# Earlier raw weights, earlier second operands, a later unpacking of w_out and a deeper fetch of c in a fused attention and two-MLP kernel

## The chip, the cores and the metric

The kernel runs on one core of a Trainium2 chip. The metric is the device time of one execution in microseconds (us), the median of several runs. Before the change it is 904.29 us over three runs (901.79 to 904.33); the execution that the profiler recorded took 901.62 us, of which 899.8 lie between its first and its last instruction.

## The reference

Three stages stand behind one another, all in float32: attention inside chunks of 64 tokens, an MLP with a leaky activation, and a bilinear MLP.

```python
scores = scale * q_c @ k_c.T                      # per chunk of 64, head size 64
x = softmax(scores) @ v_c                         # -> (2304 tokens, 512)
h = x @ w_in                                      # w_in  512 x 2048
x2 = (maximum(h, 0) + alpha * minimum(h, 0)) @ w_out      # 2048 x 512
a = x2 @ w_a;  b = x2 @ w_b                       # each 512 x 1536
out = (a * b) @ w_o                               # 1536 x 512
```

The weights arrive as 64-bit floats and are brought to 32 bits on the chip ("unpacked").

## The kernel before

**Precision.** Every float32 operand is held as two tiles, a high part (`h` at the end of the name) that ScalarE rounds and a low part (`l`) that VectorE gets by subtraction (`to_hi` L83, `to_lo` L86). A product of two operands is three matmuls: high x high, high x low, low x high.

**Stages.** The 2304 tokens are five blocks: four of 512 and one of 256. For each block, attention runs beside MLP1 of the block before it. MLP1 goes through 16 slabs j of 128 hidden columns: `s1` (12 matmuls), the activation `prelu`, and two slabs later `s2` (12 matmuls into four accumulators). At the end of a block `end1` stores the result x2 to DRAM, save for the last block, whose result stays in PSUM.

Then comes the middle stage, a = x2 w_a, b = x2 w_b and c = a*b, for 12 slabs j of 128 columns. The four blocks of 512 make two pairs, p=0 and p=1. For a pair and a slab, `pair_group` (L595) gets the four products of two blocks and two weights from seven half-size products (42 matmuls of 512 columns into three PSUM banks, psA, psB, psD) instead of eight. For that it needs sums of the token tiles, `s1` to `s4`, for each pair (`sums`, `summed`), and differences of the weight tiles, `tT`, for each slab (`weights_steps` L513, which also unpacks the two raw tiles of w_a and w_b). The block of 256, the "rest", goes through `rest_group` (24 matmuls of 256 columns into psr). Below, (p,j) is a pair group and r j a rest group. Their order is a list (`seq`, L1021): (0,0) r0 (0,1) (1,0) r1 (1,1), then (0,j) r j (1,j) for each j, and at the end (0,11) (1,11) r11. Each result c goes to DRAM.

Last comes MLP2 (L1047 on): block after block, 12 slabs each, c is loaded back, split into high and low, and multiplied with the split w_o (`s4`, three matmuls for each 128 tokens).

**What sets the order.** Every engine works through its own list in the order in which the code is written; nothing is reordered at run time. Work that is not tied to a matmul (unpacking, splitting, sums) stands in one list, `todo2`. `background(us)` takes steps from its front until their written costs reach `us`; it is called inside the loops of MLP1's last block (with the budgets `BG`, L668), twice in each pair group (2.7 and 1.2) and once in each rest group (2.0). `need` takes steps until a mark is passed. The steps for the middle stage's first operands run in MLP1's last block (`before_mlp2`), together with the unpacking of all 12 slabs of w_o (`p_steps`), whose result goes to DRAM (`pd`) and comes back just before MLP2 (`wp..l<-pd`, L1043). The second pair needs the result of the last block, so its sums can only begin after MLP1 (`late_pair`, L771).

**Buffers.** Raw weights (512 KB each), the differences `tT` and the copies out share three buffers (`stg`). 72 tiles of 128x512 (`w`) hold nearly all else. c comes back into tiles of the pools `gh` and `gl` with three buffers each. All loads and stores are issued by SyncE (SP) in one order; a store that waits for its data, or a load that waits for its buffer, holds up all that stand behind it.

Of the kernel before, what the change touches and what calls it, by code (L numbers as in the profile page):

```python
# [8 lines left out]
F32 = mybir.dt.float32  # L9
# [9 lines left out]
def chunk_attention_prelu_mlp_bilinear_mlp(  # L19
# [77 lines left out]
    units += [("p", j) for j in range(J2)] + [(m, j) for j in range(J2) for m in "ab"]  # L97
# [368 lines left out]
    X, T = {}, {}  # L466
# [14 lines left out]
    def sums(p, kk, a21, a22):  # L481

        def src(q):
            return X[p, q][kk][1].bitcast(F32)
# [28 lines left out]
    def weights_steps(j):  # L513


        th, tl = xtiles("T")
        T[j] = th.rearrange("p k n -> p (k n)"), tl.rearrange("p k n -> p (k n)")
        ua, ub = (units.index((m, j)) for m in "ab")
        gen, t = {}, {}

# [11 lines left out]
        def tt(q, a, b):  # L532
            if "t" not in t:
                t["t"] = sp.tile([P, 2 * DM], F32, tag="stg", name="tT")
            nc.vector.tensor_tensor(  # L535
                out=t["t"][:, q * Q:(q + 1) * Q], in0=a(), in1=b(), op=ALU.subtract
            )
# [4 lines left out]
        def hi(c, m):  # L542
            to_hi(T[j][0][:, c], None, t[m])

        def lo(c, m):
            to_lo(T[j][0][:, c], T[j][1][:, c], t[m])

        ca, cb, ct = slice(0, DM), slice(DM, 2 * DM), slice(2 * DM, 4 * DM)
# [5 lines left out]
            (0.0, lambda: hi(ca, "a")),  # L554
            (0.69, lambda: end(ub, "b")),
            (0.0, lambda: hi(cb, "b")),
            (0.4, lambda: tt(0, part("b", 0), part("a", 0))),
            (0.4, lambda: tt(1, part("b", 1), part("t", 0))),
            (0.4, lambda: tt(2, part("b", 1), part("b", 0))),
            (0.4, lambda: tt(3, part("a", 1), part("t", 1))),  # L560
            (0.0, lambda: hi(ct, "t")),
            (0.69, lambda: lo(ca, "a")),
            (0.69, lambda: lo(cb, "b")),
            (1.2, lambda: lo(ct, "t")),
        ]

# [98 lines left out]
    U_P = NU1  # L665
    U_AB = NU1 + J2
    early2 = {}
    BG = [0.0, 0.0] + [2.6] * 12 + [6.0, 6.0]  # L668
# [9 lines left out]
    def p_steps(j):  # L678
        i = U_P + j
        gen = {}  # L680

        def begin():
            w_dma(i + 2)
            gen[0] = unpack_ops(i, True)
            next(gen[0])
# [10 lines left out]
    def before_mlp2():  # L696
# [8 lines left out]
        def first():  # L705
            w_dma(U_P + 2)
# [18 lines left out]

        def rest_in():
# [11 lines left out]
        def p_next():  # L738
            todo2.extend(p_steps(done["p"]))
            done["p"] += 1  # L740

        done["p"] = 0
        for j in range(1, 13):
            early2.setdefault(j, []).append(p_next)
        early2[1].insert(0, first)
        for j, fn in (
            (3, lambda: sums_at(0)), (4, lambda: sums_out(0)), (5, lambda: sums_at(1)), (6, lambda: sums_out(1)),
            (8, lambda: directs(0, ("11",))), (9, lambda: directs(0, ("12",))), (10, lambda: directs(0, ("22",))),
            (11, rest_in),
            (11, lambda: (w_dma(U_AB + 2), todo2.extend(weights_steps(0)))),  # L750
            (13, lambda: (fetch(1, "11", b3, 0), fetch(1, "12", b3, 1))),
        ):
            early2[j].append(fn) if j in early2 else early2.update({j: [fn]})
# [17 lines left out]
    def late_pair(acc):  # L771
# [4 lines left out]
        steps = []  # L776
        for kk in range(2):

            def a22(kk=kk):
                t["a22", kk] = a = wtile("a22", F32)  # L780
                nc.scalar.activation(out=a, in_=acc[2 + kk], func=AF.Copy)

            t[kk], four = sums(1, kk, lambda kk=kk: acc[kk], lambda kk=kk: t["a22", kk])
            steps += [(0.0, a22)] + four
        for kk in range(2):
            steps += summed(1, kk, t[kk])
        for kk in range(2):
            hi, lo = X[1, "22"][kk]
            steps += [
# [316 lines left out]
```

## Time and profile before

| what | value |
|---|---|
| median of three runs | 904.29 us (901.79 to 904.33) |
| the profiled execution | 901.62 us, its span 899.8 us |
| PE (TensorE) busy | 864.0 us, 96% of the span |
| DVE (VectorE) busy | 525.9 us, 58% |
| ACT (ScalarE) busy | 373.5 us, 42% |
| mean granted clock of TensorE | 0.985 of full speed |

The page divides the span in 40 slices of 22.5 us; PE is full in nearly all of them:

```profile
PE   7899999999999999999996899999999969999997
PEclk9999999999999999999997999999999999999999
```

Each digit is the busy share of a slice in tenths. The slices that fall short are the first ones (attention before there is any MLP work), slices 22 and 23 (the change from MLP1 to the middle stage, 472 to 517 us), slice 33 (the change to MLP2, about 742 us) and the last. A matmul of 512 columns starts 0.227 us after the one before it at full clock and 0.43 us at half clock.

### The profile page before, as it was taken

What the parts mean: (1) busy time and instruction counts of PE and PEld (TensorE: products, weight loads), DVE (VectorE), ACT (ScalarE), POOL (GpSimd) and SP (SyncE); (2) the same over time, 40 slices, a digit from 0 to 9 for tenths busy, and PEclk for the clock granted to TensorE, in tenths of its full rate; (3) what the DMA queues carried; (4) which work ended last, traced back from release to release, by engine and by line L of the source; (5) the groups of instructions that cost most, each with busy time, mean ns of one, the idle gap of its engine ahead of it and who ended that gap; (6) DMA issues with size and microseconds to landing.
All of it is one profiled execution on the core that took longest, in us unless ns stands there. A gap on an engine that the chain in (4) does not pass through costs nothing. (4 is left out here: it accounts for less than half of the span.)

```text
span 899.8 us, 13238 instructions
## 1 busy us (share of the span) xinstructions
PE 864.0 (96%) x5154; PEld 717.5 (80%) x5154; DVE 525.9 (58%) x976; ACT 373.5 (42%) x668; POOL 0.7 (0%) x6
## 2 busy tenths in 40 slices
PE   7899999999999999999996899999999969999997
PEld 6778889988888888888774688888888858888885
DVE  5999955454434443468777677777777672322322
ACT  5687766555435433346542222222222232222222
POOL 0000000000000000000000000000000000000000
PEclk9999999999999999999997999999999999999999
DMA  9686767464425220544420523333232163434433
GB/s 212 211 249 196 211 165 176 106 162 120 116 49 162 61 59 1 187 171 165 156 77 23 168 94 105 101 101 100 100 101 76 54 217 85 146 96 142 141 91 119
DMA packets 148702, 114.12 MB, mean 127 GB/s; under 512 B 96544, under 2 KB 121120, under 8 KB 148640
## 3 DMA queue, kind: packets, MB, share of 16 engines
q1 hardware_dynamic: 148352, 113.02, 42.5%
q8 instruction: 40, 0.66, 0.3%
q10 hardware_dynamic: 288, 0.26, 0.1%
q14 instruction: 22, 0.18, 0.1%
HBM read 70.79 MB, written 34.08 MB: 117 GB/s over the span
## 5 line engine op out<-in xcount | busy, mean ns | idle before, releaser
L387 DVE SCALAR_TENSOR_TENSOR pos<-neg,nalpha_sb,pos 128x512 f32<-128x512 f32 (+1 forms) x80 | 55.6, 695 | 106.3 <-ACT pos L386 106.1
L87 DVE TENSOR_TENSOR cl<-cl,ch 128x512 fp32r<-128x512 f32 (+1 forms) x60 | 38.3, 639 | 109.1 <-ACT ch L84 103.8
L84 ACT ACTIVATE ch<-cl 128x512 fp32r<-128x512 f32 (+1 forms) x60 | 35.3, 589 | 109.4 <-DMA cl<-cd 73.2
L87 DVE TENSOR_TENSOR gl<-pos,gh 128x512 fp32r<-128x512 f32 (+1 forms) x80 | 51.0, 638 | 43.5 <-ACT gh L84 43.5
L84 ACT ACTIVATE gh<-pos 128x512 fp32r<-128x512 f32 (+1 forms) x80 | 47.2, 590 | 64.6 <-DVE pos L387 64.6
L603 DVE TENSOR_TENSOR t<-p,psB 128x512 f32<-128x512 f32 x48 | 32.8, 684 | 56.7 <-PE psB L573 55.1
L385 ACT ACTIVATE neg<-psh 128x512 f32<-128x512 f32 (+1 forms) x80 | 43.8, 547 | 35.6 <-PE psh L367 35.4
L137 DVE SCALAR_TENSOR_TENSOR wx<-wx,wz 128x512 int32<-128x512 int32 x68 | 46.7, 687 | 13.8 <-ACT wx L125 11.0
L125 ACT ACTIVATE wx<-raw 128x512 f32<-128x512 f32 x68 | 43.1, 670 | 22.7 <-DMA raw<-in_moe_w_a_dram 10.9
L607 ACT ACTIVATE p<-psA 128x512 f32<-128x512 f32 x24 | 14.3, 596 | 76.0 <-PE psA L573 75.3
L386 ACT ACTIVATE pos<-psh 128x512 f32<-128x512 f32 (+1 forms) x80 | 44.2, 552 | 0.0
L129 DVE TENSOR_SCALAR wz<-raw 128x512 uint16<-128x512 uint16 x68 | 31.3, 460 | 16.7 <-DMA raw<-in_moe_w_a_dram 9.5
L613 ACT ACTIVATE p<-psD 128x512 f32<-128x512 f32 x24 | 14.3, 597 | 47.7 <-PE psD L573 45.6
L134 DVE TENSOR_SCALAR wz<-raw 128x512 uint16<-128x512 uint16 x68 | 30.8, 453 | 0.0
L367 PE MATMUL psr<-xrh,Tl 128*128 128x256 f32 x96 | 27.2, 283 | 0.0
L367 PE MATMUL psr<-xrl,Th 128*128 128x256 f32 x96 | 27.2, 283 | 0.0
L367 PE MATMUL psr<-xrh,Th 128*128 128x256 f32 x96 | 27.1, 283 | 0.0
L243 ACT ACTIVATE kqd<-kq 128x1024 uint16<-128x1024 uint16 x24 | 23.9, 1047 | 0.3 <-DMA kq<-in_k_dram 0.3
L641 ACT ACTIVATE b_sb<-psr 128x256 f32<-128x256 f32 x12 | 4.6, 384 | 41.2 <-PE psr L367 41.2
L84 ACT ACTIVATE Th<-wx 128x512 fp32r<-128x512 f32 x24 | 15.1, 630 | 12.2 <-DVE wx L137 12.2
L84 ACT ACTIVATE xh<-psSO 128x256 fp32r<-128x256 f32 x28 | 8.9, 384 | 25.0 <-PE psSO L343 25.0
L84 ACT ACTIVATE Th<-tT 128x1024 fp32r<-128x1024 f32 x12 | 12.7, 1062 | 14.8 <-DVE tT L535 14.8
(534 smaller groups left out, 2560.1 us busy)
## 6 DMA issues: line engine op xcount, KB each, us to landing
raw<-in_moe_w_out_dram SPq DMA_DIRECT2D x28, 512.0 KB, 3.8
cl<-cd SPq DMA_DIRECT2D x48, 256.0 KB, 2.6
raw<-in_moe_w_in_dram SPq DMA_DIRECT2D x16, 512.0 KB, 5.0
raw<-in_moe_w_a_dram SPq DMA_DIRECT2D x12, 512.0 KB, 3.8
raw<-in_moe_w_b_dram SPq DMA_DIRECT2D x12, 512.0 KB, 3.6
cd<-t SPq DMA_DIRECT2D x24, 256.0 KB, 2.0
cd<-p SPq DMA_DIRECT2D x24, 256.0 KB, 2.0
v<-in_v_dram SPq DMA_DIRECT2D x16, 256.0 KB, 4.4
```

Source lines behind the costliest of these rows:

```text
L84: nc.scalar.activation(out=hi, in_=src, func=AF.Copy)
L87: nc.vector.tensor_tensor(out=lo, in0=src, in1=hi.bitcast(F32), op=ALU.subtract)
L125: return nc.scalar.activation(out=x.bitcast(F32), in_=hw.bitcast(F32), func=AF.Copy, scale=2.0 ** -112)
L129: yield nc.vector.tensor_scalar(out=z2[:, :, 0], in0=h2[:, :, 1], scalar1=13, scalar2=None, op0=ALU.logical_shift_right)
L134: yield nc.vector.tensor_scalar(out=z2[:, :, 1], in0=h2[:, :, 3], scalar1=1 << 15, scalar2=None, op0=ALU.bitwise_and)
L137: yield nc.vector.scalar_tensor_tensor(out=x, in0=x, scalar=3, in1=z, op0=ALU.logical_shift_left, op1=ALU.bitwise_or)
L243: nc.scalar.activation(out=d, in_=src.bitcast(U16).rearrange("p (f t) -> p t f", t=2), func=AF.Copy)
L367: nc.tensor.matmul(out=ps, lhsT=a, rhs=b, start=(i == 0 and first), stop=(i == n_i - 1 and a is wl))
L385: nc.scalar.activation(out=neg, in_=h, func=AF.Relu, scale=-1.0)
L386: yield nc.scalar.activation(out=pos, in_=h, func=AF.Relu)
L387: yield nc.vector.scalar_tensor_tensor(out=pos, in0=neg, scalar=nalpha_sb[:, j:j + 1], in1=pos, op0=ALU.mult, op1=ALU.add)
L603: nc.vector.tensor_tensor(out=out, in0=a, in1=b, op=op)
```

## The change

Six things are changed.

- The order in which weights are asked for (`units`) puts w_a and w_b of slabs 0 and 1 first; the 12 tiles of w_o stand between later pairs. So w_o is unpacked in the middle stage, after each (1,j), one or two tiles each, and no longer in MLP1's last block. Raw weights are asked for one slab further ahead.
- `weights_steps` is cut in two: `weights_raw` (unpacking and differences) and `weights_in` (the splits). The differences are two tiles of 512 columns in the pool `w`; they were one of 1024 in `stg`. Slab 1 gets its first half in MLP1's last block and its second half before MLP1's last products (L1012 on).
- The second pair's tokens that lie in DRAM (11 and 12) are loaded into tiles of their own (`xraw`) and split in MLP1's last block; before, after the middle stage had begun.
- `late_pair` does all of its first half (kk=0) before the second.
- In `seq`, r10 moves behind (1,11).
- c is loaded four tiles ahead, not two, into the pool `w`, and the first four loads stand between the loads of w_o.

```diff
-    units += [("p", j) for j in range(J2)] + [(m, j) for j in range(J2) for m in "ab"]
+    units += [(m, j) for j in range(2) for m in "ab"]
+    n_p = 0
+    for j in range(2, J2):
+        units += [("a", j), ("b", j)]
+        upto = min(J2, -(-(j - 1) * J2 // (J2 - 3)))
+        units += [("p", i) for i in range(n_p, upto)]
+        n_p = upto
...
-            if "t" not in t:
-                t["t"] = sp.tile([P, 2 * DM], F32, tag="stg", name="tT")
+            if q % 2 == 0:
+                t["t", q // 2] = wtile("tT", F32)
...
+    def weights_in(j):
+        names = ("a", "b", ("t", 0), ("t", 1))
...
+        return [(0.0, begin)] + stagger([
+            [(0.0, lambda i=i: to_hi(*args(i))), (0.69, lambda i=i: to_lo(*args(i)))] for i in range(4)
+        ])
...
-    BG = [0.0, 0.0] + [2.6] * 12 + [6.0, 6.0]
...
+        def raw_in():
+            for q, half in (("11", 0), ("12", 1)):
+                operand(1, q)
+                for kk in range(2):
+                    raw1[q, kk] = wtile("xraw", F32)
+                    nc.sync.dma_start(out=raw1[q, kk], in_=x2d[b3][:, 2 * half + kk])
+        def raw_out():
+            todo2.extend(stagger([settled(1, q, kk, raw1[q, kk]) for q in ("11", "12") for kk in range(2)]))
...
-        for j in range(1, 13):
-            early2.setdefault(j, []).append(p_next)
...
+            (2, first), (3, lambda: sums_at(0)), (4, lambda: sums_at(1)), (5, lambda: w_dma(NU1 + 2)),
+            (5, lambda: sums_out(0)), (6, lambda: sums_out(1)),
+            (7, lambda: directs(0, ("11",))), (8, lambda: directs(0, ("12",))), (9, lambda: directs(0, ("22",))),
+            (9, lambda: todo2.extend(weights_steps(0))), (10, lambda: w_dma(NU1 + 4)),
+            (11, raw_in), (11, rest_in), (12, raw_out),
+            (13, lambda: todo2.extend(weights_raw(1))),
...
-                    background(BG[j] if j < len(BG) else 9.0)
+                    background(2.8 if j < J1 - 1 else 3.4)
             x = nxt
+        w_dma(NU1 + 6)
+        flush(1)
         background(99.0)
-        w_dma(U_AB + 4)
         mark((0, 0))
-        todo2.extend(weights_steps(1))
+        todo2.extend(weights_in(1))
         mark((0, 1))
-        background(3.0)
+        background(99.0)
         flush(0)
         late_pair(acc[0])
         mark((1, 0))
         mark((1, 1))
+        todo2.extend(weights_raw(2))
...
-        for j in range(2, J2 - 1):
+        for j in range(2, J2 - 2):
             seq += [(0, j), ("r", j), (1, j)]
-        seq += [(0, J2 - 1), (1, J2 - 1), ("r", J2 - 1)]
+        for j in (J2 - 2, J2 - 1):
+            seq += [(0, j), (1, j)]
+        seq += [("r", J2 - 2), ("r", J2 - 1)]
...
+                todo2.extend(weights_in(j + 2))
+                mark((0, j + 2))
+                i = units.index(("b", j + 2)) + 1
+                while i < len(units) and units[i][0] == "p":
+                    w_dma(i + 1)
+                    todo2.extend(p_steps(units[i][1]))
+                    i += 1
+                w_dma(i + 2)
             if (p, j) == (0, J2 - 1):
                 for i in range(J2):
                     W["p", i] = hl = wtile(f"wp{i}h"), wtile(f"wp{i}l")
                     nc.sync.dma_start(out=hl[1].bitcast(F32), in_=pd[i])
+                    if i < AHEAD:
+                        load_c(i)
...
-            load_c(i + 2)
+            load_c(i + AHEAD)
```

On VectorE, between the last evacuation of (0,1) and the first one of (1,0), the program before had these rows; `ss` and `a` are the sums and a copied token tile, `x1..l` low parts of the second pair; (1,0)'s first evacuation comes next.

```order
L87 TENSOR_TENSOR x1s1l<-ss_5154,x1s1h 128x512
L87 TENSOR_TENSOR x1s2l<-ss_5156,x1s2h 128x512
L87 TENSOR_TENSOR x1s3l<-ss_5158,x1s3h 128x512
L87 TENSOR_TENSOR x1s4l<-ss_5201,x1s4h 128x512
L87 TENSOR_TENSOR x1s1l<-ss_5205,x1s1h 128x512
L87 TENSOR_TENSOR x1s2l<-ss_5207,x1s2h 128x512
L87 TENSOR_TENSOR x1s3l<-ss_5209,x1s3h 128x512
L87 TENSOR_TENSOR x1s4l<-ss_5232,x1s4h 128x512
L87 TENSOR_TENSOR x122l<-a_5152,x122h 128x512
L87 TENSOR_TENSOR x122l<-a_5203,x122h 128x512
L87 TENSOR_TENSOR x111l<-x111l,x111h 128x512 x2
L87 TENSOR_TENSOR x112l<-x112l,x112h 128x512 x2
```

In the same place the changed program has five of these fourteen splits, and then (1,0)'s first evacuation.

```order
L87 TENSOR_TENSOR x1s1l<-ss_5129,x1s1h 128x512
L87 TENSOR_TENSOR x1s2l<-ss_5131,x1s2h 128x512
L87 TENSOR_TENSOR x1s3l<-ss_5133,x1s3h 128x512
L87 TENSOR_TENSOR x1s4l<-ss_5135,x1s4h 128x512
L87 TENSOR_TENSOR x122l<-a_5127,x122h 128x512
L614 TENSOR_TENSOR t_5185<-p_5177,psB 128x512
```

Four of the nine others (x111l, x112l) now stand in MLP1's last block, and five (the first half, kk=0) behind (0,0) and in r0.

On SyncE, between the stores of (1,3) and those of (1,4), the program before had the following; `cd_3` and `cd_4` are stores of c for slabs 3 and 4, the last number being a buffer.

```order
L442 DMA cd_3_138<-p_5752 128x512
L108 DMA raw<-in_moe_w_a_dram 128x4x256
L108 DMA raw<-in_moe_w_b_dram 128x4x256
L442 DMA cd_4_91<-t_5826 128x512
L442 DMA cd_4_115<-p_5818 128x512
L442 DMA cd_4_103<-b_sb 128x256
L442 DMA cd_4_127<-t_5939 128x512
```

Now two raw tiles of w_o stand ahead of the pair of raw weights, and the two stores to `pd` stand among the stores of c.

```order
L448 DMA cd_3_138<-p_5691 128x512
L111 DMA raw<-in_moe_w_out_dram 128x1024 x2
L114 DMA raw<-in_moe_w_a_dram 128x4x256
L114 DMA raw<-in_moe_w_b_dram 128x4x256
L448 DMA cd_4_91<-t_5775 128x512
L448 DMA cd_4_115<-p_5767 128x512
L448 DMA cd_4_103<-b_sb 128x256
L699 DMA pd_151<-wx 128x512
L448 DMA cd_4_127<-t_5892 128x512
L448 DMA cd_4_139<-p_5884 128x512
L699 DMA pd_152<-wx 128x512
```

The second of the raw pair takes the buffer that the first raw tile of w_o leaves. On SyncE after the last store of (0,11), the loads for MLP2 were, before:

```order
L442 DMA cd_11_122<-p_7061 128x512
L1043 DMA wp0l<-pd_147 128x512
L1043 DMA wp1l<-pd_148 128x512
L1043 DMA wp2l<-pd_149 128x512
L1043 DMA wp3l<-pd_150 128x512
L1043 DMA wp4l<-pd_151 128x512
```

and are now:

```order
L448 DMA cd_11_122<-p_7071 128x512
L1068 DMA wp0l<-pd_147 128x512
L1040 DMA cl<-cd_0_87 128x512
L1068 DMA wp1l<-pd_148 128x512
L1040 DMA cl<-cd_1_88 128x512
L1068 DMA wp2l<-pd_149 128x512
L1040 DMA cl<-cd_2_89 128x512
L1068 DMA wp3l<-pd_150 128x512
L1040 DMA cl<-cd_3_90 128x512
L1068 DMA wp4l<-pd_151 128x512
```

`wp3l` was the fourth load and is the seventh; the first loads of c stood behind the stores of (1,11) and r11.

## Rows read from the trace of the kernel before

**Rows 1.** By stage: start:end, length, busy PE, PEld, DVE, ACT, POOL; clock, DMA, GB/s.

```profile
45.00:460.00 415.00, 412.05 (x2823) 345.75 (x2822) 247.46 (x487) 224.77 (x412) 0.00 (x0) 1.00 0.49 139
460.00:520.00 60.00, 47.83 (x213) 38.39 (x212) 41.86 (x71) 18.98 (x34) 0.00 (x0) 0.89 0.25 85
520.00:700.00 180.00, 180.00 (x874) 150.01 (x873) 130.47 (x228) 50.32 (x81) 0.00 (x0) 1.00 0.29 96
```

**Rows 2.** PE's waits: engine, tile, line, releaser: us in total, times, longest.

```profile
PE acc L367 <- ACT ch L84: 7.8, 2, 6.0
PE psA L573 <- ACT x111h L84: 4.6, 1, 4.6
PE psA L573 <- ACT p L607: 3.8, 2, 2.3
PE psA L573 <- DVE x111l L87: 3.6, 1, 3.6
...
PE psA L573 <- DVE Tl L87: 1.7, 1, 1.7
```

**Rows 3.** PE in order of time, MLP1's end to r2: start, duration, [idle before].

```profile
449.88 0.39 PE L573 MATMUL psA<-x011h,Th 128*128 128x512 f32 x1
...
522.74 0.28 PE L367 MATMUL psr<-xrh,Th 128*128 128x256 f32 x1
```

**Rows 4.** The chain that ended last, about (0,2): start, us, what.

```profile
519.90 1.36 PE psD L573 x6
521.26 1.65 PE psB L573 x6
522.91 2.87 PE psr L367 x24
```

**Rows 5.** VectorE in order of time, in (0,1), (1,1) and a later (0,j).

```profile
469.56 0.69 DVE L488 TENSOR_TENSOR ss<-acc,a 128x512 f32<-128x512 f32 x1 [1.12 <-ACT a L781]
...
500.86 0.46 DVE L129 TENSOR_SCALAR wz<-raw 128x512 uint16<-128x512 uint16 x1 [5.25 <-DMA raw<-in_moe_w_a_dram]
...
629.55 0.69 DVE L137 SCALAR_TENSOR_TENSOR wx<-wx,wz 128x512 int32<-128x512 int32 x1 [1.08 <-ACT wx L125]
```

**Rows 6.** VectorE in order of time, one unpacking of w_o, first and last.

```profile
430.54 0.47 DVE L129 TENSOR_SCALAR wz<-raw 128x512 uint16<-128x512 uint16 x1
...
431.44 0.69 DVE L137 SCALAR_TENSOR_TENSOR wx<-wx,wz 128x512 int32<-128x512 int32 x1
```

**Rows 7.** The chain that ended last, from (1,11) to MLP2.

```profile
726.02 4.19 DMA wp3l<-pd
...
731.59 0.61 DVE t L603
...
739.34 2.73 DMA cl<-cd
```

**Rows 8.** Busy time in the same stretch.

```profile
730.00:735.00 5.00, 3.63 (x21) 2.85 (x20) 4.68 (x8) 2.71 (x5) 0.00 (x0) 1.00 1.00 358
```

**Rows 9.** PE and VectorE in order of time there.

```profile
732.24 0.50 PE L573 MATMUL psB<-x122h,Th 128*128 128x512 f32 x1 [1.37 <-DVE t L603]
...
742.78 0.80 PE L367 MATMUL acc<-wp0h,ch 128*128 128x512 f32 x1 [5.99 <-ACT ch L84]
...
746.41 0.39 PE L367 MATMUL acc<-wp0h,ch 128*128 128x512 f32 x1
...
739.42 0.68 DVE L87 TENSOR_TENSOR wp10l<-wp10l,wp10h 128x512 fp32r<-128x512 f32 x1
740.02 0.68 DVE L87 TENSOR_TENSOR wp11l<-wp11l,wp11h 128x512 fp32r<-128x512 f32 x1
```

**Rows 10.** The chain that ended last, at the start of MLP2's block of 256.

```profile
877.04 4.03 DMA cl<-cd
```

**Rows 11.** PE in order of time there.

```profile
881.65 0.50 PE L367 MATMUL acc<-wp3h,ch 128*128 128x512 f32 x1 [1.84 <-ACT ch L84]
...
886.11 0.39 PE L367 MATMUL acc<-wp5h,ch 128*128 128x512 f32 x1
```

More of the change, by code (lines that the diff above doesn't have):

```diff
@@ L776, in late_pair, with a22 @@
         steps = []
+        def a22(kk):
+            t["a22", kk] = a = wtile("a22", F32)
+            nc.scalar.activation(out=a, in_=acc[2 + kk], func=AF.Copy)
         for kk in range(2):
-            def a22(kk=kk):
-                t["a22", kk] = a = wtile("a22", F32)
-                nc.scalar.activation(out=a, in_=acc[2 + kk], func=AF.Copy)
             t[kk], four = sums(1, kk, lambda kk=kk: acc[kk], lambda kk=kk: t["a22", kk])
[L784 to L789, printed above, removed]
-                (0.0, lambda hi=hi, lo=lo, kk=kk: to_hi(hi, lo, t["a22", kk])),
-                (0.69, lambda hi=hi, lo=lo, kk=kk: to_lo(hi, lo, t["a22", kk])),
-            ]
-        for q in ("11", "12"):
-            steps += stagger([settled(1, q, kk) for kk in range(2)])
+            out = summed(1, kk, t[kk]) + [
+                (0.0, lambda kk=kk: to_hi(*X[1, "22"][kk], t["a22", kk])),
+                (0.69, lambda kk=kk: to_lo(*X[1, "22"][kk], t["a22", kk])),
+            ]
+            steps += [(0.0, lambda kk=kk: a22(kk))] + four
+            steps += out
         todo2.extend(steps)
@@ L1052, in load_c @@
                 b, j = order[i]
-                n = sizes[b]
-                hi = gp.tile([P, NB], F32R, tag="gh", name="ch")[:, :n]
-                lo = gp.tile([P, NB], F32R, tag="gl", name="cl")[:, :n]
+                hi, lo = (wtile(nm)[:, :sizes[b]] for nm in ("ch", "cl"))
                 nc.sync.dma_start(out=lo.bitcast(F32), in_=cd[b, j])
                 cs[i] = hi, lo
-        for i in range(2):
-            load_c(i)
+        AHEAD = 4
+        left = {j: 2 for j in range(J2)}
+        for p, j in seq:
+            if p == "r":
+                rest_group(j)
+                continue
+            if j < 2 or not p:
+                need((p, j))
+            pair_group(p, j, bank if p == 0 else acc_bank)
+            left[j] -= 1
+            if not left[j] and j + 2 < J2:
+                if j:
+                    background(99.0)
+                    todo2.extend(weights_raw(j + 2))
+                todo2.extend(weights_in(j + 2))
[6 more added lines that the diff above has]
+                w_dma(i + 2)
+            if (p, j) == (0, J2 - 1):
+                for i in range(J2):
+                    W["p", i] = hl = wtile(f"wp{i}h"), wtile(f"wp{i}l")
+                    nc.sync.dma_start(out=hl[1].bitcast(F32), in_=pd[i])
+                    if i < AHEAD:
+                        load_c(i)
+                todo2.extend(stagger([settle_w(i) for i in range(J2)]))
+        background(99.0)
         for i, (b, j) in enumerate(order):
```

76 lines of the change are left out of this document (18 added, 58 removed).

## The prediction

> **What bounds the kernel now.** I read first the table by stage [rows 1]. In MLP1 (45 to 460 us) PE is busy for 412.05 of 415 us, in the body of the middle stage (520 to 700) for all of 180, both at a granted clock of 1.00. There the only way to gain is to take matmuls away, and the change takes none: every product stands as before, and in PE's order only r10 moves. Between 460 and 520 PE is busy for 47.83 of 60 us at a clock of 0.89. So the time to be won lies at the seams between stages.
>
> The second view is the list of PE's waits [rows 2]: 13.7 us for the operands of the middle stage (4.6, 3.8, 3.6, 1.7) and 7.8 us, in two waits, for c in MLP2.
>
> **The front seam.** PE begins (0,0) at 449.88 and r2 at 522.74 [rows 3]: 72.86 us for five pair groups and two rest groups. In the chain a product of six matmuls takes 1.36 us and a rest group 2.87 [rows 4]; seven products make 9.52, so the work is 5 x 9.52 + 2 x 2.87 = 53.3 us. Lost: 19.5 us, of which 13.7 are the waits above. Most of the other 5.8 is matmuls at half clock (1.2 GHz in place of 2.4) after the long ones.
>
> **The back seam.** Before the last product of (1,11) PE waits 1.37 us, before MLP2 5.99 us [rows 9]. Then nine matmul intervals take 746.41 - 742.78 = 3.63 us; at the full-clock pace of 1.36/6 they would take 2.04. Lost: 1.37 + 5.99 + 1.59 = 8.95 us.
>
> **The block of 256 in MLP2.** PE waits 1.84 us at 881.65, and the twelve matmuls up to 886.11 take 4.46 us, not 2.72 [rows 11]. Lost: 3.6 us. The chain names a load of c that took 4.03 us to land [rows 10]; it stood behind the previous block's stores.
>
> **The change, part by part**, in the order of time.
>
> **Second pair and slab 1 ready early.** The 3.8 us were waits for a copy on ACT that stood behind an unpacking whose raw weights had not landed (DVE's first step waited 5.25 us for them [rows 5]); the 4.6 and 3.6 were waits for x11. Raw weights of slabs 0 to 2 now leave SP before the middle stage, and x11, x12 and all of slab 1 are split before it. What stays there is late_pair: it needs MLP1's last accumulators and lies beside (0,0), r0 and (0,1), 9.52 + 2.87 + 9.52 = 21.9 us of PE work. Its cost on DVE: 8 sums and 10 splits, beside 14 evacuations, 32 operations at 0.60 (start of wp10l to start of wp11l [rows 9]) = 19.2 us, and DVE cannot start for 2.8 us, until the second product. That is 22.0 against 21.9, so small waits remain. In (0,1) of before the first sum started at 469.56, 5.4 us into the group, after a copy on ACT [rows 5]. Four sums then end at 7.8; the evacuation that frees psB starts there and PE gets it about 0.65 later (731.59 to 732.24 [rows 7, 9]), at 8.5 where it wants it at 8.2: 0.3 to 0.5 each in (0,0) and (0,1). In (1,0) the second half of x1s2l is ready some 3.2 us into the group and wanted at 2.3: 0.9. With 0.3 in (0,2) (next part) 2.2 us remain of the 19.5. Gain 17.3. Bounds: 19.5 if these vanish too; 13.4 if late_pair ends late by one more wait as long as the longest of before for such a copy, 2.3 [rows 2], and the slow start after it, 1.6.
>
> **Twelve unpackings of w_o move.** One takes DVE from 430.54 to about 432.05 [rows 6], 1.5 us; together 18 us leave MLP1's last block, where they were hidden, and enter the middle stage. There a period is 2 x 9.52 + 2.87 + 0.29 = 22.2 us, of which DVE works 130.47/180 x 22.2 = 16.1 [rows 1]. Nine periods take one or two unpackings each: 17.6, or 19.1. Cost: nothing, while PE covers it; without that cover 18 us. SP gets 12 loads and 12 stores in another place; the load of the second raw tile (w_b) of a slab now waits for the buffer that an unpacked w_o tile leaves, and the stores of c wait behind it. The worst is a period with two: the buffer comes free some 18 us into the period, the load needs about 4 (a smaller one took 4.03 [rows 10]), and ACT wants the weights 4.6 us into the next period, at 26.8. About 5 us of slack.
>
> **The repeating gap.** psB's last product in each (0,j) takes 1.65 us, not 1.36 [rows 4]; there are nine such pieces from 521 to 700 us. DVE's unpacking step waits 1.08 us for its partner on ACT, which stands behind an evacuation [rows 5], and the next evacuation is late by that. The new order has the same steps in the same place, so I leave the 0.29 in. The Trainium skill (Perfetto Trace Analysis, Optimization Strategy) says that the same gap repeated on the engine that should be full can mean that there are too few buffers for the next tile. By that reading the move of tT out of the three staging buffers would close the gap, and the sum would be 2.6 us lower. The row speaks against it: it names ACT as the releaser, no load and no buffer.
>
> **Loads for MLP2.** c0 to c3 now come between the first loads of w_o, so the 6 us wait for a load of c that began at 739.34 [rows 7] goes. What is late next is DVE. Before, wp3l, fourth in the queue, took 4.19 us to land [rows 7] and held up the evacuation in (1,11). Now three loads of 256 KB more are ahead of it; at 358 GB/s [rows 8] that is 3 x 0.73 = 2.2 us. The evacuation starts at 733.8 in place of 731.59, PE's wait grows from 1.37 to about 3.6. From there DVE has six evacuations, eight splits of w_o and the products of r10 and r11 before the split of c0: 14 operations of 0.60 and two of half the width, 0.3 each by estimate. So c0's low part is ready at 733.8 + 9.0 + 0.7 = 743.5, or 0.9 later if PE falls to half clock in the wait and delays an evacuation. MLP2's third matmul needs it, so MLP2 effectively starts 0.45 earlier, at 743.1 to 744.0. Before, it started at 742.78 + 1.59 = 744.4, without r10, whose 2.87 us of PE work now lie behind (1,11). Gain 744.4 - 743.1 + 2.87 = 4.2, or 3.3; I take 3.7. Bounds: 8.95 (every wait goes) and 0 (the wait only moves).
>
> **The block of 256.** Its c3 and c4 now leave SP ahead of the stores, c5 right behind them. c5 lands at 877.04 + 4.03 = 881.1 and PE wants it at 886.11 - 3.6 = 882.5. Gain 3.6. Bounds: 3.6 and, if another load is caught behind the stores, 0.
>
> **MLP1's last block.** DVE gets less work; the loads of tokens start one slab later, their sums one slab after that. PE is two slabs (10.9 us) ahead of what it needs from there. Taken as 0.
>
> Splitting tT in two tiles adds 24 small operations in places that PE covers. 0.
>
> **Sum.** 17.3 + 3.7 + 3.6 = 24.6 us. From the profiled execution's 901.62 this gives 877.0; that execution is 2.7 below the median of the runs, 904.29, from which it would be 879.7. Since the runs lie at both levels I take a value between, nearer the profile's: 878 us.
>
> **The rivals.**
>
> **Rival 1:** late_pair still ends late. For it: DVE's 22.0 us against PE's 21.9. Against it: nine gaps of 0.29 in the middle stage left the clock at 1.00 [rows 1, 4], so small waits stay small. One wait of 2.3 with its slow start, 3.9 us: 882.
>
> **Rival 2:** The back seam gains nothing. For it: wp3l falls back three places and DVE has 9 us of work after it. Against it: the long wait of before was for a load that is now long done. 878 + 3.7 = 882.
>
> **Rival 3:** The repeating gap closes, because a step that waited for one of three staging buffers no longer does: 9 x 0.29 = 2.6 us less, 875. Against it stands the releaser in the row [rows 5]. (This is what the rule of the Trainium skill named above would do here.)
>
> **Rival 4:** The middle stage turns on its raw weights (slower than before). In (1,1) of before ACT sat behind an unpacking without its raw data, and the evacuation behind that kept PE waiting 2.3 us [rows 2], with about 1.6 of slow start. If SP's longer queue made the raw weights late in every period, that is 9 x 3.9 = 35 us: 913. It decides from the point where the weights land 4.6 us after the start of (0,j), some 5 us later than I find. In two-tile periods alone (two of the remaining ones) it would be 8 us: 886.
>
> **Rival 5:** c is not really fetched deeper, because SP's order, not the buffers, holds it back, and the block of 256 keeps its wait: 881.6.
>
> **How the numbers follow.** Forecast 70%; rival 1 9%, rival 2 9%, rival 3 4%, rival 5 4%, rival 4 4% (half of it above 904). The forecast's own range is 872 (the profile's level, seams 5 us better than taken) to 883 (the median's level, 3 us worse). For 8 in 10 it reaches on to 869, where the upper bounds of all gains lie (19.5 + 8.95 + 3.6 = 32), and to 888, which takes in rivals 1, 2 and 5 at the median's level and two periods of rival 4. This kernel's measurement can tell about 0.3%, 2.7 us, from no change. Faster by more than that: 95%; within: 2%; slower: 3%.
>
> **What would show it.** Right: from (0,0) to r2 PE takes about 55.5 us and no wait of its list exceeds 1 us there; the granted clock stays at 1.00; DVE is busy for about 147 of 180 us in the middle stage and PE still for all of it; the wait before (1,11)'s last product grows to 3 or 4 us; the wait for c before MLP2 falls below 2; the one in the block of 256 is gone. Wrong: waits of psA for p or of psB for t repeated in each period (rival 4), a wait for x1s2 or x1s3 above 2 us (rival 1), a load of c named in the chain (rivals 2 and 5).

## The result, and the profile after

The changed kernel takes 878.71 us (median of 4 runs, 878.24 to 879.16), the one before 904.28 on the same chip (901.79 to 904.33): a ratio of 0.9724, 95% interval [0.9706, 0.9741]. Predicted were 878 us. The profiled execution took 878.59 us, with a span of 876.8.

The stretches between fixed points of PE's order, from PE's rows in order of time of both kernels (us; the last line is the profiled execution's time less the start of the last product):

| stretch | before | after | gain | predicted |
|---|---|---|---|---|
| start to (0,0) | 449.88 | 449.04 | 0.8 | 0 |
| (0,0) to r2 | 72.86 | 56.30 | 16.6 | 17.3 |
| r2 to r9 | 155.64 | 155.53 | 0.1 | 0 |
| r9 to MLP2's 37th product | 74.15 | 73.26 | 0.9 | 3.7 |
| 37th to last product | 143.23 | 138.54 | 4.7 | 3.6 |
| the rest | 5.86 | 5.92 | -0.1 | 0 |

The lines add up to 23.0. The prediction took the first and the last as 0; the first lies between 448.32 and 449.88 in the fourteen profiles of this case. The four between them give 22.3, where 24.6 were predicted.

The same table by stage as of before [rows 1]: start:end, length, busy PE, PEld, DVE, ACT, POOL; clock, DMA, GB/s.

```profile
45.00:460.00 415.00, 413.47 (x2834) 347.51 (x2834) 239.04 (x464) 222.75 (x409) 0.00 (x0) 1.00 0.45 119
460.00:520.00 60.00, 58.99 (x288) 48.90 (x287) 51.27 (x91) 20.44 (x37) 0.00 (x0) 1.00 0.37 130
520.00:700.00 180.00, 179.74 (x861) 149.33 (x860) 143.07 (x259) 52.91 (x97) 0.00 (x0) 1.00 0.40 134
```

From 460 to 520 PE is busy for 58.99 us, not 47.83, at a granted clock of 1.00, not 0.89. In the body of the middle stage DVE does 143.07 us of work in place of 130.47: w_o's unpackings. PE stays full.

PE's waits (engine, tile, line, releaser: us in total, times, longest); those of psA [rows 2] are gone, and those for c are down to 0.6 and 0.5.

```profile
PE psB L584 <- DVE t L614: 4.3, 4, 3.3
...
PE psB L584 <- DVE x1s2l L87: 0.7, 1, 0.7
...
PE acc L373 <- ACT ch L84: 0.6, 1, 0.6
PE acc L373 <- DVE cl L87: 0.5, 1, 0.5
```

PE in order of time, front seam (answers to [rows 3]) and back seam (answers to [rows 9]); start, duration, [idle before <- releaser].

```profile
449.04 0.39 PE L584 MATMUL psA<-x011h,Th 128*128 128x512 f32 x1
...
457.77 0.50 PE L584 MATMUL psB<-x022h,Th 128*128 128x512 f32 x1 [0.41 <-DVE t L614]
...
470.84 0.50 PE L584 MATMUL psB<-x022h,Th 128*128 128x512 f32 x1 [0.35 <-DVE t L614]
...
475.42 0.50 PE L584 MATMUL psB<-x1s2l,Th 128*128 128x512 f32 x1 [0.65 <-DVE x1s2l L87]
...
505.34 0.28 PE L373 MATMUL psr<-xrh,Th 128*128 128x256 f32 x1
...
714.40 0.80 PE L584 MATMUL psB<-x122h,Th 128*128 128x512 f32 x1 [3.31 <-DVE t L614]
...
717.13 0.41 PE L373 MATMUL psr<-xrh,Th 128*128 128x256 f32 x1
...
720.33 0.32 PE L373 MATMUL psr<-xrh,Th 128*128 128x256 f32 x1
...
725.07 0.50 PE L373 MATMUL acc<-wp0h,ch 128*128 128x512 f32 x1 [0.60 <-ACT ch L84]
...
726.29 0.50 PE L373 MATMUL acc<-wp0h,cl 128*128 128x512 f32 x1 [0.49 <-DVE cl L87]
```

The front has three waits under 0.7 us. A wait costs more than the idle time in its row: (0,0) takes 10.23 us and not 9.52 with a wait of 0.41. What is lost beyond the idle time is called the slow start. In the back seam the wait before (1,11)'s last product has grown from 1.37 to 3.31, and what follows runs at half clock (granted clock 0.50 from 714.40 to 720.33): six products take 717.13 - 714.40 = 2.73 us and not 1.36, and r10's first fifteen products 720.33 - 717.13 = 3.20, where they take 24 in 2.88 elsewhere (so 1.80). That is 2.8 us of PE's time which the prediction did not have.

The chain that ended last, there (answers to [rows 7]) and in (0,3) (answers to [rows 4]).

```profile
526.09 1.63 PE psB L584 x6
...
707.65 4.72 DMA wp3l<-pd
...
713.75 0.61 DVE t L614
```

wp3l takes 4.72 us to land. The piece of psB is 1.63 us long, as it was 1.65: the repeating gap has stayed. No load of c is left in the chain.

### The profile page after: what moved, and what is told of

It reads as the page before. It is cut to its first block, busy times and chain, and to the rows that moved or that the text cites. A ratio compares the mean times of both kernels' runs of the same rounds, so it can differ in the third digit from the quotient of the medians.

```text
span 876.8 us, 13241 instructions
## 1 busy us (share of the span) xinstructions
PE 859.0 (98%) x5154; PEld 717.9 (82%) x5154; DVE 526.1 (60%) x988; ACT 370.3 (42%) x680; POOL 0.7 (0%) x6
## 4 chain that ended last, share of the span: by engine, by line
PE 88%; DVE 8%; ACT 2%; issue 1%; DMA 1%; SPq 0%; ACTq 0%; POOLq 0%; DVEq 0%; POOL 0%
PE acc L373 38%; PE psh L373 19%; PE psB L584 11%; PE psA L584 7%; PE psD L584 7%; PE psr L373 4%; DVE wx L143 1%; PE psSO L298 1%; PE psSO L349 1%; DVE wz L135 1%; DVE ss L494 1%; DVE wz L140 1%; DMA wp3l<-pd 1%; DVE gl L87 0%; PE psT L285 0%
## 5 line engine op out<-in xcount | busy, mean ns | idle before, releaser
L461 DVE COPY os<-acc 128x512 f32<-128x512 f32 x8 | 5.5, 692 | 78.4 <-PE acc L373 78.4
L87 DVE TENSOR_TENSOR cl<-cl,ch 128x512 fp32r<-128x512 f32 (+1 forms) x60 | 35.6, 637 | 19.8 <-ACT ch L84 19.6
L84 ACT ACTIVATE ch<-cl 128x512 fp32r<-128x512 f32 (+1 forms) x60 | 33.2, 586 | 17.8 <-DMA cl<-cd 17.3
L462 ACT ACTIVATE os<-acc 128x512 f32<-128x512 f32 x8 | 4.8, 599 | 84.7 <-PE acc L373 82.2
L373 PEld LDWEIGHTS psr<-xrh,Th 128*128 128x128 f32 x96 | 19.2, 200 | 0.5
```

The lines of the kernel that those rows point to most:

```text
L84: nc.scalar.activation(out=hi, in_=src, func=AF.Copy)
L87: nc.vector.tensor_tensor(out=lo, in0=src, in1=hi.bitcast(F32), op=ALU.subtract)
L373: nc.tensor.matmul(out=ps, lhsT=a, rhs=b, start=(i == 0 and first), stop=(i == n_i - 1 and a is wl))
```

## The experiments

Each run is the changed kernel with one edit. The stretches are those of the table above.

| run | us, median | ratio to before, 95% | (0,0) to r2 | r2 to r9 | r9 to 37th | 37th to last |
|---|---|---|---|---|---|---|
| the change | 878.71 | 0.9706 to 0.9741 | 56.30 | 155.53 | 73.26 | 138.54 |
| c loaded as before | 886.21 | 0.9794 to 0.9832 | 56.27 | 155.53 | 74.59 | 143.38 |
| w_o's loads first | 873.95 | 0.9665 to 0.9702 | 56.29 | 155.52 | 69.16 | 138.56 |
| r10 back | 880.96 | 0.9737 to 0.9774 | 56.31 | 155.53 | 75.35 | 138.52 |
| early steps | 872.34 | 0.9648 to 0.9685 | 54.26 | 153.58 | 70.67 | 138.53 |
| x11, x12 late | 884.30 | 0.9765 to 0.9819 | 62.86 | 155.50 | 72.69 | 138.52 |
| slab 1 late | 882.30 | 0.9743 to 0.9798 | 60.58 | 155.47 | 73.57 | 138.53 |
| both late | 887.32 | 0.9795 to 0.9840 | 65.34 | 155.51 | 72.07 | 138.53 |
| late_pair's old order | 876.84 | 0.9681 to 0.9733 | 55.41 | 155.52 | 70.81 | 138.54 |
| w_o without DVE | 877.81 | 0.9693 to 0.9747 | 56.25 | 155.59 | 72.15 | 138.53 |
| w_o twice | 883.33 | 0.9750 to 0.9815 | 58.04 | 159.07 | 72.19 | 138.52 |
| new back seam | 870.66 | 0.9614 to 0.9656 | 56.33 | 155.54 | 65.36 | 138.51 |
| early steps, new back seam | 866.25 | 0.9564 to 0.9606 | 54.29 | 153.58 | 65.00 | 138.54 |

**The front: x11 and x12.**

```
-            return raw1[q, kk] if p else X[p, q][kk][1].bitcast(F32)
+            return X[p, q][kk][1].bitcast(F32)
...
-            (11, raw_in), (11, rest_in), (12, raw_out),
+            (11, rest_in),
...
+            (13, lambda: (fetch(1, "11", b3, 0), fetch(1, "12", b3, 1))),
 # and at the end of late_pair's steps
+        for q in ("11", "12"):
+            steps += stagger([settled(1, q, kk) for kk in range(2)])
```

> The change with x11 and x12 of the second pair split where they were before: loaded in slab 13 and split behind all sums of late_pair. My theory: late_pair then has 36 operations of 0.60 us on DVE and not 32, and the first product of (1,0), which reads x11, stands behind all of them, 22.0 + 2.4 us and not 21.9 after the start of (0,0): a wait of 1 to 3 us at the start of (1,0) and a slow start after it, 881 to 884. Rival, that x11 and x12 alone were all of the front seam (the two waits for x111h and x111l of before, 8.2 us, and their slow starts): over 887. Rival, that slab 1 alone was: 878.7.

Measured: 884.30, 5.6 above the change and just beyond what was expected; the wait is 5.10 us, not 1 to 3. PE in order of time:

```profile
477.39 0.79 PE L584 MATMUL psA<-x111l,Th 128*128 128x512 f32 x1 [5.10 <-DVE x111l L87]
```

The product is the second of (1,0) and runs at half clock (0.79). The size was off because 32 operations do not follow each other without stops. DVE's rows of the change show it: after the start at 452.03 DVE waits twice for late_pair's copy on ACT, 1.78 and 1.72 us, and once 0.72 for PE, so its last split ends 28 us after (0,0)'s start and not 22; the waits are 4.2 of the 6 us.

```profile
452.03 0.69 DVE L614 TENSOR_TENSOR t<-p,psB 128x512 f32<-128x512 f32 x1 [5.22 <-PE psB L584]
454.50 0.69 DVE L494 TENSOR_TENSOR ss<-acc,a 128x512 f32<-128x512 f32 x1 [1.78 <-ACT a L789]
...
467.57 0.69 DVE L494 TENSOR_TENSOR ss<-acc,a 128x512 f32<-128x512 f32 x1 [1.72 <-ACT a L789]
...
476.48 0.69 DVE L87 TENSOR_TENSOR x122l<-a,x122h 128x512 fp32r<-128x512 f32 x1
```

**The front: slab 1.**

```
-            (9, lambda: todo2.extend(weights_steps(0))), (10, lambda: w_dma(NU1 + 4)),
+            (9, lambda: todo2.extend(weights_steps(0))),
...
-            (13, lambda: todo2.extend(weights_raw(1))),
...
-        w_dma(NU1 + 6)
+        w_dma(NU1 + 4)
-        todo2.extend(weights_in(1))
+        todo2.extend(weights_steps(1))
-        background(99.0)
+        background(3.0)
+        todo2.append((0.0, lambda: w_dma(NU1 + 6)))
         todo2.extend(weights_raw(2))
```

> The change with slab 1's raw weights asked for behind MLP1's first product of the last slabs and unpacked in the middle stage's first groups, as before; those of slab 2 follow them. My theory: ACT and DVE stand behind an unpacking whose raw weights have not landed, as before (a wait of about 4 us and a slow start of 1.6), and late_pair is later by the 4 us that the unpacking takes on DVE, which PE's 21.9 us no longer cover: 884 to 888. Rival, that slab 1 is hidden there: 878.7.

Measured: 882.30, 3.6 above and below the 884 to 888 expected; the front is 4.28 longer. The waits are late_pair's, not the unpacking's:

```profile
475.38 0.80 PE L584 MATMUL psB<-x1s2h,Th 128*128 128x512 f32 x1 [2.77 <-ACT x1s2h L84]
...
477.12 0.79 PE L584 MATMUL psB<-x1s2l,Th 128*128 128x512 f32 x1 [0.95 <-DVE x1s2l L87]
```

(0,0) itself takes 9.52 us here, its work without a wait, so the raw weights held up nobody there; x1s2 was 2.77 and 0.95 us late in (1,0), and what follows runs at half clock (0.80). The second half of the theory stands, the first does not: late_pair is later, though by less than 4 us (x1s2l is ready 28.7 us after (0,0)'s start, 26.3 in the change).

**The front: both.** The two edits above together.

> The change with both parts of the front undone together: x11 and x12 of the second pair loaded in slab 13 and split behind late_pair's sums, and slab 1's raw weights asked for and unpacked at the start of the middle stage. Each alone lengthens the stretch from the first product of (0,0) to r2, 56.30 us with the change, by 6.56 and 4.28 us. My theory: the two stand in one queue on DVE ahead of (1,0), so together they cost more than their sum, and the stretch goes back to what it was before the change, 72.86: 878.7 + 16.6 = 895. Rival, that they add up and the rest of the front's gain is late_pair's new order: 878.7 + 10.8 = 889.5.

Measured: 887.32, 8.6 above: neither the theory's 895 nor the rival's 889.5, but nearer to the rival. The wait for x111h grows to 7.06 us, and all the loss is ahead of r1:

```profile
478.22 0.79 PE L584 MATMUL psA<-x111h,Th 128*128 128x512 f32 x1 [7.06 <-ACT x111h L84]
...
480.13 0.80 PE L584 MATMUL psA<-x111l,Th 128*128 128x512 f32 x1 [1.12 <-DVE x111l L87]
```

From (0,0) to r1 PE took 44.11 us before, 34.06 with the change, 43.12 here; from r1 to r2 28.75, 22.24 and 22.22. So the two edits explain 9.1 of the first stretch's 10.1 us. They overlap (9.1 and not 10.8): PE's only waits up to r1 are these two, at one place. The other 6.5 us of the front's 16.6 lie between r1 and r2, where before DVE waited 5.25 us for slab 2's raw weights [rows 5]; here these were still asked for in time. That this alone gave the 6.5 was not tried.

**The front: late_pair's order.**

```
-            steps += [(0.0, lambda kk=kk: a22(kk))] + four
-            steps += out
+            steps += [(0.0, lambda kk=kk: a22(kk))] + four
+        for kk in range(2):
+            steps += summed(1, kk, t[kk])
+        for kk in range(2):
+            steps += [
+                (0.0, lambda kk=kk: to_hi(*X[1, "22"][kk], t["a22", kk])),
+                (0.69, lambda kk=kk: to_lo(*X[1, "22"][kk], t["a22", kk])),
+            ]
```

> The change with late_pair's steps in the order of before: the sums of both halves first, then the splits of both, the splits of x22 last; x11 and x12 stay ahead. My theory: the same steps fit in the same places beside 21.9 us of PE work; the second half's sums come sooner and the splits that (1,0) wants later, x122l and x1s4l last of all: a wait of about 1 us more in (1,0), 878.7 to 880. Rival, that this order carried what the two other parts of the front do not explain (16.6 - 10.8 = 5.8 us): 884.5.

Measured: 876.84, 1.9 below: both theories fall. The front is 0.9 shorter: with all sums ahead DVE waits for the copy on ACT once (1.78) and not twice, the waits of 0.35 in (0,1) and 0.65 in (1,0) go, and one of 0.43 for x122h comes. So the change's new order of late_pair cost a little. The other difference lies in the back seam, where this edit changes nothing:

```profile
713.93 0.50 PE L584 MATMUL psB<-x122h,Th 128*128 128x512 f32 x1 [3.31 <-DVE t L614]
...
715.42 0.28 PE L373 MATMUL psr<-xrh,Th 128*128 128x256 f32 x1
```

The same wait of 3.31 us, but the next six products take 1.49 us, at full clock (granted clock 1.00 from 700 us to 735); r9 to the 37th product takes 70.81 and not 73.26. This execution took 875.69 us; the slowest of this kernel's four took 878.05.

**w_o without and with twice its unpackings.**

```
 # without: the loads, the widening and the stores stay
-        return [(0.0, begin), (0.46, go), (0.46, go), (0.69, end)]
+        return [(0.0, begin), (0.69, store)]
 # twice: a first unpacking whose result is dropped stands ahead
+        return [(0.0, begin), (0.46, again), (0.46, again), (0.69, again),
+                (0.0, start), (0.46, go), (0.46, go), (0.69, end)]
```

> The change without three of the four steps of each of w_o's twelve unpackings (those on DVE; the loads, the widening on ACT and the stores stay, so w_o's values are wrong). My theory: what the unpackings cost DVE in the middle stage, 18 us, is hidden by PE, so nothing comes back: 878.7, within 1. Rival, that DVE's load makes the repeating gap: the pieces of 1.63 us become shorter and 2.6 us come back, 876.

> The change with each of w_o's twelve unpackings done twice in the middle stage. My theory: a period of 22.2 us has 17.4 us of DVE work with one unpacking and 19.4 with two; twice as many make 18.9 and 22.3. The periods with one stay as they are; the three with two reach the end of the cover and cost 0 to 2 us each: 879 to 885. Rival, that the unpackings stand in the way of the evacuations wherever they are: each of the nine periods is longer by what is added, 12 x 1.5 = 18 us, 897.

Measured: 877.81 and 883.33. Without the unpackings r2 to r9 takes 155.59 (155.53 with them), and so the pieces are not shorter: they cost nothing there. The 0.9 us come from the back seam, where the half clock is shorter (six products in 2.08 us), which this edit did not aim at. Twice as many cost 4.6 us; in the profile it is 5.3 up to r9, all in the periods with two tiles. Busy time in three periods of the run with twice as many, the first and last of them with two tiles:

```profile
482.90:506.90 24.00, 22.54 (x109) 18.50 (x108) 21.84 (x42) 8.32 (x15) 0.00 (x0) 1.00 0.59 195
506.90:529.10 22.20, 22.20 (x109) 18.56 (x108) 19.10 (x36) 7.08 (x13) 0.00 (x0) 1.00 0.44 153
551.30:575.30 24.00, 22.54 (x109) 18.50 (x108) 21.84 (x42) 8.32 (x15) 0.00 (x0) 1.00 0.36 115
```

A period with one tile holds 19.1 us of DVE work and keeps its 22.2 us; one with two holds 21.84, which 22.2 us would hold only if DVE never stopped for ACT or PE, and grows to 24.0 (three such, 1.76 each on the mean). So the cover ends somewhere between 19.1 and 21.84 us of DVE work in a period of 22.2. The change itself comes to 19.1 in its own periods with two tiles, 17.7 in the others.

**The repeating gap.**

```
         product(D, p, "s1", j, 4, True)
+        while todo2 and todo2[0][0] == 0.0:
+            todo2.pop(0)[1]()
         p5 = tmp(tp, "t", "p5")
```

> The change with those steps of the list that cost DVE nothing (copies and widenings on ACT) issued ahead of the copy of psD in each pair group, where they stand first in the list. My theory: the repeating gap of 0.29 us per period is DVE waiting for a widening on ACT that stands behind that copy; with the widening first the long pieces of 1.65 us go (nine of them), and so do the waits of 0.41 and 0.35 in (0,0) and (0,1), which stand behind a copy of the accumulators in the same way: 9 x 0.27 + 0.76 = 3.3 us less, 875.4. Rival, that the gap is a lack of buffers or DVE's load: the pieces stay at 1.63 and the time at 878.7.

Measured: 872.34, 6.4 below. From r2 to r9 1.95 us go, seven times 0.28. ScalarE and VectorE in order of time, in (0,3): first the change, then the run with the early steps.

```profile
522.05 0.60 ACT L624 ACTIVATE p<-psD 128x512 f32<-128x512 f32 x1 [2.12 <-PE psD L584]
522.54 1.21 ACT L131 ACTIVATE wx<-raw 128x512 f32<-128x512 f32 x2
...
523.22 0.69 DVE L143 SCALAR_TENSOR_TENSOR wx<-wx,wz 128x512 int32<-128x512 int32 x1 [1.09 <-ACT wx L131]
```

```profile
517.57 1.20 ACT L131 ACTIVATE wx<-raw 128x512 f32<-128x512 f32 x2
519.80 0.60 ACT L626 ACTIVATE p<-psD 128x512 f32<-128x512 f32 x1 [1.03 <-PE psD L584]
...
520.00 0.69 DVE L143 SCALAR_TENSOR_TENSOR wx<-wx,wz 128x512 int32<-128x512 int32 x1
...
523.84 1.36 PE psB L584 x6
```

In the change the two widenings on ACT stand behind the copy of psD, and DVE waits 1.09 us for the first. With the widenings ahead it does not wait, and psB's last piece takes 1.36 us. The front is 2.0 shorter (1.0 expected, with (0,2)'s piece: the slow starts go too, and the wait in (1,0) falls to 0.45). The other 2.6 us come from the back seam, where 0.3 was expected: the wait there falls to 1.93 and no half clock follows. One wait is new, for a copy of psD that now stands behind a copy of a w_o tile not yet landed:

```profile
PE psD L584 <- ACT p L626: 1.3, 1, 1.3
```

**The back seam: c loaded as before, w_o's loads first, r10 back.**

```
 # c loaded as before: AHEAD = 2, tiles from gp, and
-                    if i < AHEAD:
-                        load_c(i)
+        for i in range(AHEAD):            # behind background(99.0) of the last group
+            load_c(i)
 # w_o's loads first
-                    if i < AHEAD:
-                        load_c(i)
+                for i in range(AHEAD):
+                    load_c(i)
 # r10 back
-        for j in range(2, J2 - 2):
+        for j in range(2, J2 - 1):
...
-        seq += [("r", J2 - 2), ("r", J2 - 1)]
+        seq += [(0, J2 - 1), (1, J2 - 1), ("r", J2 - 1)]
```

> The change without one part: c is loaded two ahead, into the buffers of the pair groups, and its first loads are issued behind the stores of r10 and r11, as before the change. My theory: the wait in the block of 256 comes back (3.6 us), wp3l is fourth in the queue again, so the wait before the last product of (1,11) falls from 3.31 to about 1.4 us, and a wait of some us for c before MLP2 takes its place: 882 to 886 (by the two terms of the prediction, 3.7 + 3.6, it would be 886). Rival, that c was not held up by its place and its buffers: 878.7, no change. A second rival, that the back seam's gain is r10's move alone: 878.7 + 3.6 = 882.3.

> The change with c0 to c3 loaded behind all twelve loads of w_o and not between them. My theory: wp3l is fourth in the queue again, so the wait before (1,11)'s last product falls from 3.31 to 1.4 us or less, the half clock after it (2.8 us in six long and fifteen short matmuls) goes, and DVE's chain to the split of c0 starts 2.2 us earlier; DVE then sets the start of MLP2, some 2.5 us earlier: 876. Rival, that PE's own losses count in full (1.9 + 2.8): 874. Rival, that c lands too late from there: a wait for c before MLP2 of over 3 us, 879 or more.

> The change with the rest group r10 back ahead of (0,11), so that only r11 lies between (1,11) and MLP2. My theory: DVE's splits of w_o, not PE, set the start of MLP2, so r10's 2.87 us of PE work are no longer hidden there; DVE has one short product less to do: 878.7 + 2.9 - 0.3 = 881.3. Rival, that the seam is set by PE's own work and its wait for wp3l: 878.7.

Measured: 886.21, 873.95 and 880.96. With c as before (just above the range, at the two terms' 886), 4.8 us come back behind the 37th product and 1.3 in the seam; a wait of 5.1 us before MLP2 takes the place of the one in (1,11), which falls to 2.09. Its waits:

```profile
PE acc L373 <- ACT ch L84: 6.9, 2, 5.1
PE psB L584 <- DVE t L614: 3.1, 4, 2.1
```

With w_o's loads first the time is that of the rival that counts PE's losses in full (874), and the seam is 4.1 us shorter, not 2.5. PE in order of time:

```profile
712.01 0.50 PE L584 MATMUL psB<-x122h,Th 128*128 128x512 f32 x1 [1.71 <-DVE t L614]
...
713.52 0.28 PE L373 MATMUL psr<-xrh,Th 128*128 128x256 f32 x1
...
721.45 0.50 PE L373 MATMUL acc<-wp0h,cl 128*128 128x512 f32 x1 [0.69 <-DVE cl L87]
```

A wait of 1.71 us, then full clock (0.50 and not 0.80; six products in 1.51). But it is not PE's losses that count. I had taken DVE's chain, from its evacuation ahead of (1,11)'s last product to c0's split, as fixed. VectorE's rows, first of the change, then of this run:

```profile
713.66 0.68 DVE L614 TENSOR_TENSOR t<-p,psB 128x512 f32<-128x512 f32 x1
...
725.55 0.68 DVE L87 TENSOR_TENSOR cl<-cl,ch 128x512 fp32r<-128x512 f32 x1
```

```profile
711.27 0.68 DVE L614 TENSOR_TENSOR t<-p,psB 128x512 f32<-128x512 f32 x1
...
720.72 0.68 DVE L87 TENSOR_TENSOR cl<-cl,ch 128x512 fp32r<-128x512 f32 x1
```

The chain takes 725.55 - 713.66 = 11.89 us in the change, and here 720.72 - 711.27 = 9.45: DVE waits for (1,11)'s last product, and by way of ACT's copies for r10's and r11's, and these come sooner at full clock. So the half clock cost DVE's chain 2.44 us, and the earlier evacuation gives the other 1.65 of the 4.1. The sum holds beyond these two: in the nine profiles with the change's order of groups and of w_o's splits and without a late load of c, the time from r9 to that evacuation, this chain and 8.57 to 8.59 us more make up the stretch from r9 to the 37th product. With the early steps, too, the chain takes 9.45.

With r10 back 2.25 us are lost, 2.6 expected, and PE waits first for ACT's and then for DVE's part of c0's split: DVE's chain, not PE, sets MLP2's start.

```profile
716.62 0.80 PE L584 MATMUL psB<-x122h,Th 128*128 128x512 f32 x1 [3.40 <-DVE t L614]
...
724.66 0.50 PE L373 MATMUL acc<-wp0h,ch 128*128 128x512 f32 x1 [2.15 <-ACT ch L84]
...
726.80 0.80 PE L373 MATMUL acc<-wp0h,cl 128*128 128x512 f32 x1 [1.41 <-DVE cl L87]
```

**A better version.** The back seam in another order, alone and with the early steps.

```
-                    if i < AHEAD:
-                        load_c(i)
-                todo2.extend(stagger([settle_w(i) for i in range(J2)]))
+                    if i == AHEAD - 1:
+                        for c in range(AHEAD):
+                            load_c(c)
+            if (p, j) == (1, J2 - 1):
+                todo2.extend(stagger([settle_w(i) for i in range(AHEAD)]))
 # ahead of r11
+                    split(*cs[0], cs[0][1].bitcast(F32))
 # in MLP2's loop, behind load_c(i + AHEAD)
+            if i + AHEAD < J2:
+                todo2.extend(settle_w(i + AHEAD))
+                background(99.0)
```

> The change with another back seam: c0 to c3 are loaded behind the first four loads of w_o, no split of w_o stands in (1,11), the first four stand behind it, c0's split goes ahead of r11, and the other eight stand one by one beside MLP2's first slabs. My theory: (1,11) waits for no load, DVE has seven evacuations, four splits of w_o and c0's ahead of MLP2 beside r10's and r11's 5.7 us, so the seam's losses (3.31 of wait, 2.8 at half clock, 1.1 of waits before MLP2) nearly all go: 878.7 - 6.5 = 872. Rival, that the splits between MLP2's slabs come too late for PE: waits of acc for wp of over 1 us each in the first block, 875 or more.

> The back seam of the run beside it together with the steps that cost DVE nothing issued ahead of the copy of psD. My theory: the two are independent but for what each takes from the seam: the stretch from (0,0) to r9 as with the early steps alone (207.8 us and not 211.8), the seam as in the run beside it: 867 to 868. Rival, that an early step on ACT waits for a load of w_o in (1,11) and holds up the copy of psD, as it did with the early steps alone (1.26 us): 869 or more.

Measured: 870.66 and 866.25, each about a microsecond below what was expected. Both beat the change; the second is 12.5 us below it (ratio to before 0.9585 [0.9564, 0.9606]). The seam is 7.9 us shorter: PE goes from (1,11) through r10 and r11 into MLP2 without a wait. Busy time in the first of them, then PE in order of time in the second, where 0.45 in (1,0) and 0.26 in (1,10) are the only waits from (0,0) to the end:

```profile
700.00:720.00 20.00, 20.00 (x112) 17.56 (x111) 13.81 (x23) 7.35 (x15) 0.00 (x0) 1.00 0.77 275
```

```profile
473.54 0.50 PE L584 MATMUL psB<-x1s2l,Th 128*128 128x512 f32 x1 [0.45 <-DVE x1s2l L87]
...
687.11 0.50 PE L584 MATMUL psB<-x122h,Th 128*128 128x512 f32 x1 [0.26 <-DVE t L614]
```

## Why the prediction was right

**The front seam** (17.3 predicted, 16.6 measured). The mechanism holds: undoing the two parts brings back 9.1 us, and the remaining waits are the ones that were worked out: 0.41 and 0.35 for psB (0.3 to 0.5 predicted), 0.65 for x1s2l (0.9). The comparison of DVE's 22.0 us with PE's 21.9, on the other hand, was wrong: DVE ends after 28 us, since it stops for ACT. It cost little only because what late_pair makes last, x122l, is wanted last in (1,0); the prediction did not work that out, so this part of its success is luck. Of the gain, 6.5 us (r1 to r2) are argued from the raw weights' wait and not shown by a run.

**w_o's unpackings and the raw weights** (0 predicted, 0.1 measured). Shown from both sides: taking them out gives nothing back between r2 and r9, twice as many cost only in the periods that then hold 21.84 us of DVE work. Rival 4 did not come: no period is longer than 22.2 us.

**The repeating gap** (0 predicted, 0 measured). Rival 3 fell with the change itself: tT no longer takes a staging buffer, and the piece is 1.63 us. The early steps then closed it with not one buffer more. The Trainium skill (Perfetto Trace Analysis, Optimization Strategy) says that such a repeated gap can mean too few buffers; here it did not, and the releaser in the row, ACT, led to the cause: a copy that stood ahead of the widening.

**The back seam** (3.7 predicted, 0.9 measured) is the term that was mis-sized. The steps came as worked out: PE waits 3.31 (3.6 predicted), MLP2's waits for c are 0.60 and 0.49 (under 2). But the step that followed, that PE would at worst delay one evacuation by 0.9 if it fell to half clock, sized the loss too small. The half clock made DVE's chain 11.89 us long; in the run with late_pair's old order, where it did not follow the same wait of 3.31, the chain took 9.45 and the seam 70.81, 2.45 less. So the half clock cost 2.44, not 0.9. Even without it the gain is 3.3 and not the 4.2 worked out for that case: the evacuation came some 0.25 later than worked out, and the chain was 9.45 and not 9.0. By the size alone this is near rival 2 (nothing gained), but not by its cause.

**The block of 256** (3.6 predicted, 4.7 measured behind the 37th product). Its wait and slow start are gone, and with c as before they are back (143.38). The other 1.1 us are mostly gaps of 0.1 to 0.2 us that I had not listed, at 785 us and in that block, where products of before follow each other at 0.29 to 0.39 us and not 0.23; they too are back with c as before.

**The other rivals.** Rival 1 did not come: no wait for late_pair exceeds 0.65 us. Nor did rival 5: no load of c stands in the chain, and loading c as before costs 4.8 us behind the 37th product.

In the sum the back seam's 2.8 us and the front's 0.7 too much stand against 1.1 too little in the block of 256 and the start's 0.8: 1.6 us, from 877.0 by the profile's level to the 878.59 measured. That the forecast of 878 is within 0.7 us is so in part luck: misses of 3.5 and 1.9 us stand against each other, and 1.0 had been added because the runs of before lie at two levels. Of the signs, two came only in part: the clock did not stay at 1.00 (0.50 behind the wait in (1,11)), and DVE's 143.07 us stand against 147.

## What to carry to other kernels

At a seam, find the chain that sets its length, here DVE's, and work out what the lower clock behind a wait costs that chain and not only the engine that waited. A stop that repeats in each period is first a question of who stands ahead of the releaser in its own queue: moving a cheap step ahead of a copy won 6.4 us, 4.0 of them between (0,0) and r9, and 4.4 on top of the new back seam, a sixth of what the whole change did. And preparatory splits can be spread into the stage that uses them, one per slab, in place of standing all ahead of its first product; here that came together with another order of the loads and an earlier split of c0 (8.0 us in all), and no run parts the three.

## What the hardware showed

The clock after the wait before (1,11)'s last product, from PE's rows of the twelve profiles that have one. After the shorter waits, 1.37, 1.71, 1.93 and 2.09 us, the six products behind took 1.49 to 1.51 us: full clock, four of four. After the longer ones, of 3.31 to 4.08 us, they took 2.72 or 2.73 us in five of eight (half clock throughout), 2.08 and 2.23 in two and 1.49 in one. So a wait of over 3 us did not always bring the half clock: 3.31 us did in the change and did not in the run with late_pair's old order, whose program is the same there. Nor are the four shorter ones a safe length: elsewhere a wait of 1.84 us (in MLP2's block of 256 before [rows 11]) and one of 2.77 us (in (1,0) with slab 1 late) were followed by a granted clock of 0.50. And the fall can come after the wait is over: in the first of these PE goes on at 881.65 us, and the granted clock is 1.00 up to 882.47 and 0.50 from there to 885.88. A prediction can carry such a loss only as a bound.
